# Retention and mixer kernel: 28 causal masks as ScalarE copies with a GpSimd select, 13 sums moved to GpSimd, and another instruction order

## The chip, the cores and the metric

The kernel runs on one core of one Trainium2 chip. A core has a matrix engine (TensorE, PE in the profile), a vector engine (VectorE, DVE), an activation engine (ScalarE, ACT), a general engine (GpSimd, POOL) and a queue engine (SyncE, SP). Each takes its own instructions strictly in the order in which they were written, and waits at an instruction whose inputs are not there. The metric is the device time of one execution in microseconds (us). The time before is the median of three runs, 188.34 us (188.1 to 188.44).

## What is computed

Two layers follow each other. The first is a recurrent retention over 4 batches, 8 heads, 768 positions and head size 64; the second is a token and channel mixer with a 256-wide token part and a 1536-wide channel part.

```python
for t in range(S):
    state = gamma[None, :, None, None] * state + np.einsum('bhd,bhe->bhde', k[:, :, t], v[:, :, t])
    y[:, :, t] = scale * np.einsum('bhd,bhde->bhe', q[:, :, t], state)
...
xt = x.transpose(0, 2, 1)
h = np.maximum(xt @ w_tok1, 0.0) @ w_tok2
u = x + h.transpose(0, 2, 1)
h2 = np.maximum(u @ w_ch1, 0.0) @ w_ch2
return (u + h2).astype(np.float32)
```

`x` is `y` with the heads side by side, 768 x 512 per batch. Inputs, weights and the output are float32.

## The kernel before

The recurrence is computed in chunks of 128 positions. Within a chunk, scores of keys against queries are masked so that a query sees no later key; between chunks a decayed state is carried. The front part (`front(b, p)`) runs once per batch and pair of heads, 16 times. It scales k by the decay (L343, L345), turns q and k (L377, L379, or a transposing transfer, L367), makes the state sums (L408, L418, L420) and their diagonal blocks (L434, L436), the scores (L453), the masks (L463), the products of masked scores with v and of queries with the state (L474, L483), and then the token part of the mixer (L489 to L541), which leaves `u` as float16 for the next products and as float32 in `X`.

A lot of scores is three chunks of one head, a PSUM bank of 128 x 384 float32. A pair has four lots. VectorE multiplies each by the 0/1 mask and writes float16 `am` (L463); six `am` buffers go round. Two lots together feed one group of L474.

The back part (`back(b)`) runs once per batch and is the channel part. Batches 0 and 1 widen with plain products (L606, evicted at L622 by ScalarE); batches 2 and 3 with seven instead of eight block products (`widen7`, L647 to L725). All narrow with seven products where two row blocks are taken together (`narrow7`): sums of blocks (L784), products into three banks (L820 `chain`, L830 `tail`), three partial results kept in SBUF (`us`, L810, "keep"), and adds into `X` (L837, "add"). Of the adds, some read a bank (`FROM_BANK`), one reads one kept quarter (`y11`, 128 x 256, `FROM_KEPT`), and one reads two kept quarters at once (`y2`, 128 x 512). When its adds are done a row block is sent out (L862). Batch 3 ends with two plain blocks (L746, L755, L761).

The order of everything is written out beforehand: `PLAN` is a string, and `placed` reads it. An operation is two base-62 digits, its number in the order of creation; then a digit if it has several possible engines ("ways"), then one digit for each PSUM bank that it takes. A `+` with a digit stands for that many filler matmuls on zeros (L935). Engines, banks and order thus all come from the string; each engine's queue is the string cut down to its own operations. GpSimd's queue holds the requests of weights and of batch 0 and 1's inputs (L257, L292, L295) and casts of v (L360).

Of the kernel before, what the change touches and what calls it, by code (L numbers as in the profile page):

```python
# [11 lines left out]
ALU = mybir.AluOpType  # L12
# [9 lines left out]
class Op:  # L22
# [15 lines left out]
DIGITS = "0123456789abcdefghijklmnopqrstuvwxyzABCDEFGHIJKLMNOPQRSTUVWXYZ"  # L38

PLAN = (  # L40
    "000b09010704020f0d1h00a031i10506+e1n0+31l11o1j20e1p081m1q0c1W31X1k0+31w121A1v451r1x1S0+42x30g1T1+21U41V0+42642"
    "1y0h0k1s2y1z0i2730292t11B51Y11t01Z1E61u02b2u00j201C281F2v21D0212w0+42H242a2c0222J232z32K1G02A240+12I212501H41I"
    "2L2d0m1J02f22g0l2B2M2C2e03812h02D2E390n0p2Q43413511N2i32F02G02j1K2k02N12O0r2P12l2R1L01O01M13630E2o3a72m03712T5"
    "2S02n01P00q2U3b2p03c3d3e2V03i033L61Q53k3f2q03g03j023l3h03n3m0u0o2W2X02Z0t3M2r33o20s3p2Y03013r00v3q03s4k13H13t0"
    "3I11R03u63v2s13w04l3273J53300x3x3A3N70w5s33y03D13B03F3z10z0yaC23C0aF03G13E0aDbc1bdbe5taEbf33O3K0bg3P3Qbl6bh311"
    "3R4g13S4h1aGbi2bmaHbn3V57413W3Y4m33Z0A3T04nbjaL0aMbk4i4aI2aNaJ4300F3X4074j04o3U1aK4u4156bA2410D0C0B4p444q4wbB"
    "4x4rbCb91b05b1421451b32ba4634P0b24Q14y474804v4T64V44cbJ3494a0bKb44s14Ubb4b0bL1d4W4X4R6b54YaU54S14C1aO7aP5o04d0"
    "aQbr3b624z6b74Z1f504t1b8bsaX74f4e14AaV4B0aR24DaS0G511aY521btaW535304aTaZbx21e4F74E154570Kby0I5p0bM4G4H0bu4bG5"
    "bvbo7bw565q04IbzbHbD25r0bNbO550H4J015bEbS0bQ31716bPbFbIbp0R5b55c602582bq59c8184Lcc7bR1bT5a05d04K05e45f5g1620"
    "4M04N01b631cd00L5Y0ce6bX0bY5Z0bV5hbW0c9cb5u15i065466bZch640J4O617M16A2cf67c005v5j07N0ci0685wcac4c1695x5k5yc25z"  # L50
    "5l0cl5m0cu5C10266a0N5Dcv5Ecy5cA4cj1cB0M6b0cm06C05A0cz1c5cq5F5H4cD5B05I6c0cE05Gcr6d62306gck5K75J05LcH5M05N36D0"
    "5O6hcn5P05Q5ncwcx0S0Q5R06f6l3c36ecI15TcF26m5U0cG5W6cM5X15V06EcN6y16i76j6z0dL6cJdq5cK5S1cocZ0dMdU27K16BdVdrcQ1"
    "dscRd84dNdW781cL19d96k1d00Pdk26F6790cS0OdR5dS6G6H6Id16n06JbU6K6o06p1ada1ccT46q0dO10T6L1dPcU6rdl7I17c0dQdT6s07b"
    "6t1d51dm7d16M07a2d6dw56N72066ud76Qdb16O6Rdcdd7J00VdX0dYdZ6P6v17edF76V18i1dn2dxdycV6W7O7f07g7P6dG6S56T8j0dHdo"
    "dh46U0di7hcg7icW77j6X07k6Y07Q7R6Z7Sdp7Ldz27l07008m1cpdjdAdB6w1cX717217T0U731cY74de2dfdg7n7340dt5du7U7p750d22d3"
    "7r7o8n06xdv760d47qdI07X75367v4e07s20X7V081e2e17m0dC18k2807YdD7t7wdJdE7W17u07x0dKeb67y1eIeJeK7Z1geceL7z850e470W"
    "7A08U00Ye507E7Be617C07F0e9cs18258o8S1eO3e38T0cCef837G07D0868Z2eg8l8W18p4ea0908qed7He79112840eM68818reP8s870e8"
    "89ee0ei8X18t92938a08e8ueh8beN08c08VeT177eU8d094ej8f0eRemeQes5eS0eteVen8x72438zeq5eo8h8Yc61eXeW09w08B11ct113er0"
    "8v08y9x00Z10a428AeYf0f19u2evew0f4epex7f5ey8w0ezf86cP08g0eueA0c708C18D970432989bf9eBfc8F08GeCfm28E0999aeD8I7f6"
    "fdcO08H0eEfa3fb8J950eFf7eZfnfo48K0961fffgfe78LfqfD5fh9c3fkfrfpfEa218M0ftfH9dfifAfja319y8N0fl9s19t19f49g9v149e0"  # L60
    "f219h08Ofu8P0fs68R9i18Q1fv9jfF79k0fy9lfGa90aa9z1fz9o9A9m0fIabfw9Bac9C9p09q0gm7fx9DadfKfJ2gnfR4fLgqfP9Eae9n0fS"
    "f319H0316fCfM9L9KfVfNfQg85fT69F0go1fO9Ja5grfWgtfX2fYgpfU9Ig9gs1gugcfZgvg09G0ge6ga0gbg5g39M3gAgdg6gfgy9Na60gggh"
    "9P09O09Qg1g2gwgxg79R0gkgigja709S29TgCfB9U0glgzg4gDgH19Y9VgI19W0gJ5gBgFgKgEaf0gZh34a89Z09X0gO7h0ah3526ajala1ai"
    "h40gMel09rh8gN0eH0gPh1akgQa01h90hcag0am3anha6ao0ap2gGhd1as0aqek0ar0gR1gSgVhbh2heathhau0avaw0hlgThmhfayhnh56az0"
    "hoh6h7hghp0hHax0hr3hw6hq0gWhxgLhuhZ1aBhshv0gUhAhL3i0ig7hyhIhMhti3hN5hihBgX0hz0hPhChKhDi4i6hOihhQhF0hJiki16ii5"
    "iu4hSi2ijidi7i56hR5ibhEhTilhUi8hXinhVicaA0hYiL0im1hWi9j55ioisipiaiviZ3ieiw2itiqiMirixiyizj17j0iN6iPgY0iBj3iQj4"
    "iIiOj2iR2iA6iSk67iCiDeG1jdiTj6j7iGjY1j8iJjbiXiUjeiHiEiYjcifjCj9jG4jEjajZk7k8iViFhj1hk1iWiKk0jfjgjN5k9jk2kahG0"
    "k1kbk2k3jDjOjRke6jH0jLjM0jijr3k4kckd1jPjFjl0jhjSk50jpjq0jI5jQ1jTjW1jsjJjtjvjjjKjwju0jm5jxjUjnjVjojykfkgkhjA0"
    "jX0kijzjB0kjkkkl0"
)  # L70


# [24 lines left out]
def kernel(  # L97
# [11 lines left out]
    nc = tc.nc  # L109
# [48 lines left out]
    def dve(n, per=1.04, extra=0):  # L158
        t = int(65 + extra + n * per)
        return t, t + 83  # L160
# [153 lines left out]
    def front(b, p):  # L314
# [37 lines left out]
        if b in PLAIN:  # L352
            VF, V = V, Slot("v")

            def emit(e):
                t = tile_of(V, [P, 2, NC, D], F16)
                if e == "ACT":
                    nc.scalar.copy(t, VF.tile)
                else:
                    (nc.vector if e == "DVE" else nc.gpsimd).tensor_copy(t, VF.tile)  # L360
# [97 lines left out]
                    [SC[g] for g in run], [KT, QT], tiled="row")  # L458
            score_ops.update({g: a2 for g in run})
        for g, lot in enumerate(lots):  # L460
            def emit(g=g, m=len(lot)):
                am = tile_of(AM[g], [P, m, P], F16)
                nc.vector.tensor_tensor(am, SC[g].tile[:, :m * P].rearrange("p (i t) -> p i t", t=P),  # L463
                                        mask.to_broadcast([P, m, P]), ALU.mult)
# [121 lines left out]
    def back(b):  # L586
# [178 lines left out]
        def narrow7(i0, i1):  # L765
# [14 lines left out]
            for j, (x, y, f, d, prev) in enumerate(sums):  # L780
                def emit(e, j=j, x=x, y=y, f=f):
                    if HS.tile is None:
                        tile_of(HS, [P, 4, K2, P], F16)
                    (nc.vector if e == "DVE" else nc.gpsimd).tensor_tensor(HS.tile[:, j], x(), y(), f)  # L784
# [50 lines left out]
            def add(dst, b_, deps, uses, ways):  # L835
                def emit(e):
                    (nc.vector if e == "DVE" else nc.gpsimd).tensor_tensor(dst(), dst(), b_(), ALU.add)  # L837
# [130 lines left out]
```

## Time and profile before

| | us |
|---|---|
| median of three runs | 188.34 |
| the profiled execution's own time | 188.52 |
| its span, first to last instruction | 186.7 |
| ScalarE's busy time | 122.1 |
| GpSimd's busy time | 33.6 |

The granted TensorE clock was 1.000. In the profile a line such as "L463 DVE TENSOR_TENSOR am<-bank,mask ... x64 | 33.4, 552 | 1.5" is a group: line of the code, engine, operation, what it writes and reads, how many; then busy time in us, the mean length of one in ns, and the engine's idle time just before them. The chain is followed back from the last instruction, at each step to what released it. A stretch row of the view by stretches has the stretch, its length, then for each engine its busy time and in brackets its instructions. Matmuls overlap in the pipeline, so the time that each adds is read from the distance of their starts.

### The profile page before, as it was taken

The page shows a single profiled execution, that of the slowest core. Times are in us where ns is not written, and L with a number is a line of the kernel's source. Part 1 is how long each engine was busy: PE and PEld are TensorE (multiplying, and loading weights), DVE is VectorE, ACT ScalarE, POOL GpSimd, SP SyncE. Part 2 cuts the span into 40 slices and gives each one's busy share as a digit, 9 for nine tenths or more (in the row PEclk, how much of TensorE's full clock was granted, in tenths as well). Part 3 has the DMA queues.
Part 4 walks back from the last instruction along what each step waited for, and adds up shares of the span by engine and source line. Part 5 has one row for each costly group of instructions (what it writes and reads, how often), then busy time and mean ns, then how long its engine had stood idle before and what let it go on. Part 6 is the DMA issues. An engine that isn't in the chain of part 4 may idle for free.

```text
span 186.7 us, 5207 instructions
## 1 busy us (share of the span) xinstructions
PE 178.8 (96%) x2075; PEld 134.9 (72%) x2075; DVE 167.7 (90%) x434; ACT 122.1 (65%) x279; POOL 33.6 (18%) x44
## 2 busy tenths in 40 slices
PE   7888999999999899999999999999999999999992
PEld 3445988677679779765768888776588986566782
DVE  3799998899999799889889999999999999879982
ACT  3837998856779676287988667689875254882110
POOL 8995676420001010001010000021000000000000
PEclk9999999999999999999999999999999999999999
DMA  8999999999999999999999959997926344011025
GB/s 113 154 171 195 178 176 178 185 187 205 190 183 217 183 230 167 148 226 205 131 228 234 162 101 215 312 192 171 157 42 146 111 140 185 2 58 58 32 112 197
DMA packets 94233, 30.23 MB, mean 162 GB/s; under 512 B 84352, under 2 KB 91264, under 8 KB 94208
## 3 DMA queue, kind: packets, MB, share of 16 engines
q1 hardware_dynamic: 61840, 17.63, 53.6%
q0 software_dynamic: 30208, 8.46, 43.8%
q10 hardware_dynamic: 2160, 3.80, 5.6%
q8 instruction: 16, 0.26, 0.6%
q14 instruction: 9, 0.07, 0.1%
HBM read 26.74 MB, written 6.29 MB: 177 GB/s over the span
## 4 chain that ended last, share of the span: by engine, by line
PE 59%; DVE 25%; DMA 6%; ACT 6%; issue 2%; POOL 0%; DVEq 0%; POOLq 0%; ACTq 0%
PE bank L606 15%; PE bank L820 9%; PE bank L679 9%; PE bank L830 7%; DVE am L463 5%; DVE X L837 4%; DMA row<-in_q_dram 4%; PE bank L503 4%; PE bank L523 3%; DVE U L420 3%; DVE hs L784 3%; PE bank L746 3%; DVE h L696 3%; DMA v<-in_v_dram 2%; PE bank L453 2%
## 5 line engine op out<-in xcount | busy, mean ns | idle before, releaser
L606 PE MATMUL bank<-uT,wc 128*128 128x384 f16 x192 | 36.4, 326 | 0.0
L463 DVE TENSOR_TENSOR am<-bank,mask 128x384 f16<-128x384 f32 x64 | 33.4, 552 | 1.5 <-PE bank L453 1.4
L622 ACT ACTIVATE h<-bank 128x384 f16<-128x384 f32 x48 | 22.0, 500 | 10.0 <-PE bank L606 9.8
L606 PEld LDWEIGHTS <-wc 128*128 128x128 f16 x192 | 17.3, 98 | 9.1 <-issue 0.2
L696 DVE TENSOR_TENSOR h<-bank,us 128x384 f16<-128x384 f32 x36 | 18.8, 553 | 2.0 <-ACT us L691 1.0
L691 ACT COPY us<-bank 128x384 f32<-128x384 f32 x36 | 16.6, 484 | 6.1 <-PE bank L679 2.2
L820 PEld LDWEIGHTS <-hs 128*128 128x128 f16 x198 | 18.8, 98 | 2.5
L810 ACT COPY us<-bank 128x256 f32<-128x256 f32 x26 | 9.6, 374 | 16.2 <-PE bank L820 13.8
L360 POOL CAST v<-row 128x768 f16<-128x768 f32 x6 | 5.0, 826 | 82.9 <-DMA row<-in_v_dram 53.6
L837 DVE TENSOR_TENSOR X<-X,bank 128x256 f32<-128x256 f32 x44 | 17.9, 417 | 1.0 <-PE bank L830 0.9
L420 DVE SCALAR_TENSOR_TENSOR U<-U,gp,bank 128x64 f32<-128x64 f32 x64 | 16.8, 278 | 0.8
L820 PE MATMUL bank<-wsum,hs 128*128 128x256 f16 x132 | 17.2, 273 | 0.0
L529 ACT CAST u<-bank 128x384 f16<-128x384 f32 x29 | 13.7, 491 | 4.1 <-PE bank L523 3.4
L679 PE MATMUL bank<-hs,wsum 128*128 128x384 f16 x72 | 15.1, 326 | 0.1
L434 ACT ACTIVATE diag<-U,gp 64x320 f16<-64x320 f32 x24 | 13.3, 559 | 2.6 <-DVE U L420 2.3
L523 PE MATMUL bank<-h,wt 128*128 128x128 f16 x192 | 14.8, 219 | 0.0
L489 ACT CAST x<-bank 128x384 f16<-128x384 f32 x27 | 12.2, 488 | 3.0 <-PE bank L483 2.9
L503 PE MATMUL bank<-x,wt 128*128 128x128 f16 x192 | 13.8, 219 | 0.2 <-DVE U L418 0.2
L830 PEld LDWEIGHTS <-h 128*128 128x128 f16 x132 | 12.5, 98 | 1.9
L679 PEld LDWEIGHTS <-wsum 128*128 128x128 f16 x96 | 9.1, 98 | 5.7 <-issue 0.4
L503 PEld LDWEIGHTS <-wt 128*128 128x128 f16 x192 | 11.9, 98 | 1.9 <-DMA wt<-in_moe_w_tok_dram 0.4
L523 PEld LDWEIGHTS <-wt 128*128 128x128 f16 x192 | 12.1, 98 | 1.2
(91 smaller groups left out, 364.4 us busy)
## 6 DMA issues: line engine op xcount, KB each, us to landing
out_dram<-X ACTq DMA_DIRECT2D x14, 256.0 KB, 2.3
row<-in_q_dram SPq DMA_DIRECT2D x8, 384.0 KB, 4.9
row<-in_v_dram SPq DMA_DIRECT2D x8, 384.0 KB, 5.1
row<-in_k_dram SPq DMA_DIRECT2D x8, 384.0 KB, 5.5
wc<-in_moe_w_ch_dram POOLq DMA_DIRECT2D x5, 512.0 KB, 13.3
out_dram<-X SPq DMA_DIRECT2D x9, 256.0 KB, 3.2
v<-in_v_dram POOLq DMA_DIRECT2D x8, 192.0 KB, 9.3
row<-in_q_dram POOLq DMA_DIRECT2D x8, 192.0 KB, 8.6
```

What stands on the lines that cost most here:

```text
L420: nc.vector.scalar_tensor_tensor(out=u[:, c], in0=u[:, c - 1], scalar=gp[:, p:p + 1], in1=st, op0=ALU.mult, op1=ALU.add)
L463: nc.vector.tensor_tensor(am, SC[g].tile[:, :m * P].rearrange("p (i t) -> p i t", t=P), mask.to_broadcast([P, m, P]), ALU.mult)
L503: nc.tensor.matmul(acc[:, jt * P:(jt + 1) * P], wt1[:, i, jt * P:(jt + 1) * P], X16.tile[:, i], start=(i + jt == 0), stop=(i == NC - 1), s ...
L523: nc.tensor.matmul(Y[hf].tile[:, i * P:(i + 1) * P], wt2[:, jt, t], H1.tile[:, jt], start=False, stop=(jt == NJ - 1), skip_group_check=True)
L606: nc.tensor.matmul(acc[:, :SH], wc1[:, ct, ft * P:(ft + 1) * P], UT.tile[:, ct, sh * SH:(sh + 1) * SH], start=(ct == 0), stop=(ct == NP - 1))
L622: nc.scalar.activation(H2.tile[:, ft], A.tile[:, :SH], AF.Relu)
L679: nc.tensor.matmul(acc[:, :SH], left(ct), r[:, ct], start=first and ct == 0, stop=ct == 1, skip_group_check=True)
L691: (nc.scalar.copy if e == "ACT" else nc.vector.tensor_copy)(kept(j), A.tile[:, :SH])
L696: nc.vector.tensor_tensor(into(hf)[:, ft], bank.tile[:, :SH], kept(j), ALU.add)
L820: nc.tensor.matmul(acc_[:, lo], l[:, j], r[:, j], start=first and j == 0, stop=j == K2 - 1, skip_group_check=True)
L830: nc.tensor.matmul(acc_[:, lo], l[:, j], r[:, j], start=first and j == 0, stop=j == K2 - 1, skip_group_check=True)
L837: (nc.vector if e == "DVE" else nc.gpsimd).tensor_tensor(dst(), dst(), b_(), ALU.add)
```

## The change

For batches 1 to 3 (`CHOSEN`) each of the 48 masks gets two ways: VectorE's product as before, or a plain copy by ScalarE from the bank to `am`, followed by a GpSimd operation that sets the later keys to zero in place (`affine_select`). For a mask that the plan leaves to VectorE, GpSimd's operation puts out no instruction. The readers of `am` now depend on that second operation. The adds of kept results (`y11`, `y2`) get GpSimd as a second way.

The plan is another string throughout. Read with `placed`'s rules, it gives 28 of the 48 masks to ScalarE with GpSimd (9, 7 and 12 in batches 1, 2 and 3), and 13 adds of kept results to GpSimd: 7 of one quarter and 6 of two. Of the other operations that can run on either, 48 go from ScalarE to VectorE and 35 from VectorE to ScalarE (decays, diagonals, evictions); among the casts of v, two go from GpSimd and two to it. Filler matmuls are 45 instead of 35. Six output transfers go from ScalarE's queue to SyncE's, two the other way.

```diff
@@ PLAN @@
-    "000b09010704020f0d1h00a031i10506+e1n0+31l11o1j20e1p081m1q0c1W31X1k0+31w121A1v451r1x1S0+42x30g1T1+21U41V0+42642"
...
+    "00010302050406090b1h00f1i108070d+e1j01k11n11o0a1p1q0e1r1S01s+51l01m0h+71v011W21T11x1y+51Y11w031t01u01X1Z0c0g"
...
@@ settings @@
+    CHOSEN = (1, 2, 3)
@@ front @@
-            def emit(g=g, m=len(lot)):
+            by = []
+
+            def emit(e, g=g, m=len(lot), by=by):
                 am = tile_of(AM[g], [P, m, P], F16)
-                nc.vector.tensor_tensor(am, SC[g].tile[:, :m * P].rearrange("p (i t) -> p i t", t=P),
-                                        mask.to_broadcast([P, m, P]), ALU.mult)
-            am_ops.append(op(one("DVE", dve(len(lot) * P), emit), [score_ops[g], mask_op], [AM[g]], [SC[g]]))
+                sc = SC[g].tile[:, :m * P].rearrange("p (i t) -> p i t", t=P)
+                by.append(e)
+                if e == "ACT":
+                    nc.scalar.copy(am, sc)
+                else:
+                    nc.vector.tensor_tensor(am, sc, mask.to_broadcast([P, m, P]), ALU.mult)
...
+            am_ops.append(op(either(emit, DVE=dve(len(lot) * P), ACT=act(len(lot) * P)), [score_ops[g], mask_op],
+                             [AM[g]], [SC[g]]))
+
+            def emit(g=g, m=len(lot), by=by):
+                if by[0] == "ACT":
+                    nc.gpsimd.affine_select(out=AM[g].tile, in_=AM[g].tile, pattern=[[0, m], [1, P]],
+                                            compare_op=ALU.is_ge, fill=0.0, base=0, channel_multiplier=-1)
+            am_ops[-1] = op([("POOL", 600, 700, emit)], [am_ops[-1]], [], [AM[g]])
+            am_ops[-1].chosen_by = am_ops[-1].deps[0]
@@ narrow7 @@
-            FROM_BANK, FROM_KEPT = dict(DVE=(331, 414)), dict(DVE=(335, 418))
+            FROM_BANK, FROM_KEPT = dict(DVE=(331, 414)), dict(DVE=(335, 418), POOL=(660, 760))
...
-                     dict(DVE=(606, 690)))
+                     dict(DVE=(606, 690), POOL=(1220, 1320)))
```

More of the change, by code (lines that the diff above doesn't have):

```diff
@@ L46 @@
[L46 to L60, printed above, removed]
@@ L66 @@
[L66 to L69, printed above, removed]
+    "00010302050406090b1h00f1i108070d+e1j01k11n11o0a1p1q0e1r1S01s+51l01m0h+71v011W21T11x1y+51Y11w031t01u01X1Z0c0g"
+    "1U41V00k2t0+42642201A210l222u01z2735282x623291E01B41C0i2b2y3812c22v51F392a2402502w01D00j3402d0m0n+32H562J2K2z1"
@@ L70 @@
+    "jL5iUjhjcjdiViWjyiXjkjN7jMjR1jz6jOjljAjBjPji7jniZjQjCjjjm6jSjD7jejoiYjEhK1j1jsjTjFjtkK4jJjZj0jfjKjXjpjujvjUjV"
+    "jqkLjGjYk0jrkoir1fO1f70jwjWjHkS5kTkUkVl06kWkMkNks1jIkOkt0k1k2kqkpkPkxk3k67kQk70kR1i51k4kXk5kz4kd0ky0kYkAkZ1kB"
+    "ku5kC1kDkekbkc0kEkvkrkhkfkg0kGk85kikF0kw1kkl1l2l3kj1kHk9kI0kJ0ka1km0kll4l5kn0l6l70"
 )
@@ L460, in front @@
         for g, lot in enumerate(lots):
-            def emit(g=g, m=len(lot)):
+            by = []
+            def emit(e, g=g, m=len(lot), by=by):
                 am = tile_of(AM[g], [P, m, P], F16)
-                nc.vector.tensor_tensor(am, SC[g].tile[:, :m * P].rearrange("p (i t) -> p i t", t=P),
-                                        mask.to_broadcast([P, m, P]), ALU.mult)
-            am_ops.append(op(one("DVE", dve(len(lot) * P), emit), [score_ops[g], mask_op], [AM[g]], [SC[g]]))
+                sc = SC[g].tile[:, :m * P].rearrange("p (i t) -> p i t", t=P)
[4 more added lines that the diff above has]
+                    nc.vector.tensor_tensor(am, sc, mask.to_broadcast([P, m, P]), ALU.mult)
+            if b not in CHOSEN:
+                am_ops.append(op(one("DVE", dve(len(lot) * P), lambda f=emit: f("DVE")), [score_ops[g], mask_op],
+                                 [AM[g]], [SC[g]]))
+                continue
+            am_ops.append(op(either(emit, DVE=dve(len(lot) * P), ACT=act(len(lot) * P)), [score_ops[g], mask_op],
+                             [AM[g]], [SC[g]]))
+            def emit(g=g, m=len(lot), by=by):
[4 more added lines that the diff above has]
+            am_ops[-1].chosen_by = am_ops[-1].deps[0]
         Y = [Slot(FA) for _ in range(2)]
```

34 lines of the change are left out of this document (25 added, 9 removed).

## The prediction

> **What bounds the kernel now.** I read the page first: its span, the busy shares, then the chain that ended last.
>
> ```profile
> span 186.7 us, 5207 instructions
> ...
> PE   178.8 (96%) x2075; PEld 134.9 (72%) x2075; DVE 167.7 (90%) x434; ACT 122.1 (65%) x279; POOL 33.6 (18%) x44
> ...
> PE 59%; DVE 25%; DMA 6%; ACT 6%; issue 2%; POOL 0%; DVEq 0%; POOLq 0%; ACTq 0%
> ```
>
> TensorE looks full, VectorE stands at 90%, and a quarter of the last chain is VectorE. So the first question is which of the two sets the time. A matmul's shown length includes its pipeline, so busy time says little; the spacing of matmuls in unbroken runs says more. The chain in order of time has such runs, the first wide matmuls of the back part, and VectorE's stretch:
>
> ```profile
> 31.46 3.72 PE bank L606 x22
> ...
> 71.51 0.67 PE bank L503 x12
> ...
> 76.76 3.90 PE bank L606 x24
> ...
> 97.25 0.56 DVE hs L784
> ...
> 98.27 0.93 DVE hs L784 x2
> 99.20 0.93 DVE am L463 x2
> ...
> 132.29 0.47 DVE h L696
> ...
> 141.45 0.44 PE bank L453 x12
> ...
> 179.71 1.31 PE bank L830 x12
> ```
>
> A 384-column matmul costs 3.90/24 = 0.163 us of TensorE, a 256-column one 1.31/12 = 0.109, a 128-column one 0.67/12 = 0.056, a score 0.44/12 = 0.037; a mask or a six-block sum costs VectorE 0.93/2 = 0.465, less than its shown length. Next, how many matmuls there are after 40 us, when the loads are over: the busy time by stretch for L606, L679, L820, L830, L503 and L523 alone, one row each in this order.
>
> ```profile
> 40.00:186.70 146.70, 29.39 (x155) 13.71 (x153) 1.00 0.86 160
> ```
> ```profile
> 40.00:186.70 146.70, 30.88 (x168) 15.96 (x168) 1.00 0.86 160
> ```
> ```profile
> 40.00:186.70 146.70, 34.60 (x264) 24.91 (x264) 1.00 0.86 160
> ```
> ```profile
> 40.00:186.70 146.70, 26.19 (x198) 18.78 (x198) 1.00 0.86 160
> ```
> ```profile
> 40.00:186.70 146.70, 10.49 (x144) 9.19 (x144) 1.00 0.86 160
> ```
> ```profile
> 40.00:186.70 146.70, 11.17 (x144) 9.20 (x144) 1.00 0.86 160
> ```
>
> 323 x 0.163 + 462 x 0.109 + 288 x 0.056 = 52.6 + 50.4 + 16.1 = 119.1 us. The smaller groups, from the groups of TensorE between 40 and 183.5 us:
>
> ```profile
> L474 PE MATMUL bank<-v,am 128*128 128x64 f16 x132 | 7.3, 193 | 0.0
> L746 PE MATMUL bank<-wc,h 128*128 128x256 f16 (+1 forms) x36 | 6.5, 308 | 0.0
> L483 PE MATMUL bank<-diag,qT 128*128 128x128 f16 x55 | 6.3, 219 | 0.0
> ...
> L453 PE MATMUL bank<-qT,kT 64*128 64x128 f16 x120 | 5.1, 217 | 1.3 <-DVE U L420 0.7 <-DVE X L539 0.4 <-PE bank L483 0.3
> ```
>
> By columns these are about 3.7 (half of a 128-column one each), 5.2 (24 of 256 columns, 12 of 512), 3.1 and 4.4, and for the groups left out I put 3.4: 20 us. Together 139 us of work in a stretch of 143.5. So **TensorE is the bound after 40 us and idles about 4.5 us there**, although the chain lies almost wholly on VectorE from 97 to 133 us: other batches' matmuls stand ready and fill in. That caps what relief of VectorE can bring. The change removes no matmul. The rest is the ramp before 40 us, which hangs on loads, and the end:
>
> ```profile
> 183.46 0.42 DVE L755 TENSOR_TENSOR X<-X,bank 128x256 f32<-128x256 f32 x1 [0.51 <-PE bank L746]
> 183.91 0.34 ACTq L761 DMA_DIRECT2D out_dram<-X  x1
> ```
>
> From the last matmul to the end of the span are 3.3 us: an add, an issue, a transfer.
>
> **The change part by part.** The durations, from the groups of instructions by form:
>
> ```profile
> L463 DVE TENSOR_TENSOR am<-bank,mask 128x384 f16<-128x384 f32 x64 | 33.4, 552 | 1.5 <-PE bank L453 1.4
> ...
> L837 DVE TENSOR_TENSOR X<-X,us 128x512 f32<-128x512 f32 x11 | 7.6, 690 | 0.3
> ...
> L837 DVE TENSOR_TENSOR X<-X,us 128x256 f32<-128x256 f32 x11 | 4.6, 422 | 0.1
> ```
> ```profile
> L529 ACT CAST u<-bank 128x384 f16<-128x384 f32 x29 | 13.7, 491 | 4.1 <-PE bank L523 3.4 <-ACT us L810 0.7
> ```
> ```profile
> L360 POOL CAST v<-row 128x768 f16<-128x768 f32 x6 | 5.0, 826 | 82.9 <-DMA row<-in_v_dram 53.6 <-PE bank L523 17.1 <-PE bank L453 10.3
> ...
> L212 POOL IOTA us<- 128x384 f32 x1 | 0.5, 455 | 0.0
> L192 POOL IOTA away<- 128x128 f32 x1 | 0.2, 228 | 0.4 <-POOLq L952 0.4
> ```
>
> *VectorE.* 28 masks of 0.552, 7 quarter sums of 0.422 and 6 half-row sums (two quarters each) of 0.690 leave: 15.5 + 3.0 + 4.1 = 22.6 us, or about 19.1 when each gives 0.087 back to its neighbour, as the mask does (0.552 against 0.465). The new plan also moves evictions and scalings between ScalarE and VectorE: 48 to VectorE, 35 back, net 13, some 5.4 us at 0.42. VectorE's net relief is near 14 us.
>
> *ScalarE.* 28 copies of a 384-column bank at 0.49 are 13.7 us, less 13 leaving operations of about as much each, 6.4: 122 becomes 129 of 187. It has room; a copy frees the score bank as early as the mask did.
>
> *GpSimd, the select.* No row shows one. Its floor is the 384-column iota, 0.455 us. The two iotas give 0.114 + 0.89 us per 1000 columns, and the cast beyond that fixed part (0.826 - 0.114)/768 = 0.93; index and data one after the other make 0.114 + 384 x 1.82/1000 = 0.81. I take 0.6. *The sums.* One operand at the cast's rate is 0.35 for 256 columns and 0.59 for 512 (0.83 for 768 is the row); two operands one after the other 0.59 and 1.06. I take the upper ends, as both operands come through one engine. 28 x 0.6 + 7 x 0.59 + 6 x 1.06 = 27.3 us; GpSimd goes from 34 to 61 us. The Trainium skill, "GPSIMD Engine Reference", section Elementwise — side-by-side cycle accounting, gives about 2.6 cycles per element for two inputs; an estimate by it is 0.67 and 1.22 us, 1.5 us more over the 13 sums, and no run here shows one yet.
>
> *What is queued behind.* After a copy the select waits on GpSimd's own queue, behind weight and batch-1 load issues until 40 us, later behind casts and sums, and TensorE's in-order queue waits at L474 for it. In the new list, TensorE work between the end of the scores and the reader of a chosen mask is at least 2.3 us (by the planner's matmul costs, close to the spacings above), and between the place of the copy and that reader at least 1.5; copy and select need 0.49 + 0.6 = 1.1, so each fits if nothing stands in front. Nine of the 28 selects are listed within 0.7 us of their reader. There I charge 0.07 us on average, 0.6 in all; at worst they lose 0.6 each, 5.4. The sums are waited for by output transfers only, and by the last transfers of batch 3.
>
> *The shared lock.* While a cast ran, VectorE was held twice. First row of each pair GpSimd, second VectorE:
>
> ```profile
> 66.17 0.83 POOL L360 CAST v<-row 128x768 f16<-128x768 f32 x1 [7.47 <-DMA row<-in_v_dram]
> ```
> ```profile
> 66.42 0.98 DVE L784 TENSOR_TENSOR hs<-hs,h 128x768 f16<-128x768 f16 x1
> ```
> ```profile
> 84.12 0.83 POOL L360 CAST v<-row 128x768 f16<-128x768 f32 x1 [17.13 <-PE bank L523]
> ```
> ```profile
> 84.11 1.04 DVE L345 TENSOR_SCALAR k<-row,gk 128x384 f16<-128x384 f32 x1
> ```
>
> The sum at 66.42 ended at 67.40, 0.41 after the cast at 67.00: it had waited for it, for about 0.43 (such a sum beside it is 0.93/2 plus overlap, 0.55). The scaling lost about 0.6. Masks and bank adds beside other casts kept their length. Two of six casts cost VectorE 1.0 us, 0.17 per cast. 41 more instructions, somewhat shorter, make some 6 us; VectorE's net relief falls from 14 to 8. The Trainium skill, "SBUF — State Buffer", section Who interferes with whom, says that VectorE instructions with two SBUF inputs, and its two-port modes, exclude GpSimd's reads for a whole instruction, first come first served; that speaks against this change and the two rows agree with it.
>
> *Fillers and tail.* The plan has 45 filler matmuls for 35; 10 x 0.163 = 1.6 us in the ramp, counted at nothing where TensorE waits for loads, 1.6 if not. In the tail three GpSimd sums (0.59 + 1.06 + 0.59 = 2.2 us) must be done before ScalarE's queue may issue the last transfer. By the list their inputs are ready about 5, 2.5 and 1.3 us before the last matmul ends; run in that order they end before it: nothing, at worst 0.6.
>
> *Sum.* Of the 4.5 us that TensorE idles after 40 us, I give half to VectorE's lateness: -2.3. Late selects: +0.6. Ramp and tail: 0. Net -1.7 us on the span, 185.0. The profiled execution took 188.52, 1.8 more than its span, so 186.8; it lies 0.2 above the median of 188.34, so **186.6 us** for the median.
>
> **The rivals.** (1) *Late selects: slower.* GpSimd's queue becomes a latency in front of TensorE. If a select takes 1.0 instead of 0.6, or a 1.06 us sum stands in front of it, the nine tight ones lose 0.4 to 0.6 us each: 9 x 0.5 = 4.5, less the 2.3 gained, is +2.2, 190.5. It decides when GpSimd's part exceeds about 0.9 us. For: TensorE's queue is in order and full. Against: GpSimd now idles 82% of the span, and the selects may run ahead of their place in the list. (2) *The lock, slower.* Were every one of the 41 to hold a VectorE instruction for its whole length, as two casts did for half to three quarters of theirs, VectorE would lose 27 us and gain 14: 13 us worse than now. TensorE hides most of it (now it idles 4.5 us while VectorE is a quarter of the chain, 47 us); a quarter, 3 us, would show: 191.3. Against: four of six casts held nothing. The Trainium skill's rule on that page is this rival's mechanism. (3) *Nothing.* The 4.5 us idle are transfers and hand-offs, not VectorE's load (the L453 row names a VectorE U, a VectorE X and TensorE itself, 0.3 to 0.7 us each); then -0.3 to +0.3, 188.3. (4) *More.* The new order also tightens the ramp, and most of the 4.5 us go: -4.3, 184.0. That the select is left out cannot be: the place of each select asks which engine the copy was given.
>
> **How the numbers follow.** Forecast (-0.4 to -3.0 us, 185.3 to 187.9) 0.45; late selects 0.22; lock 0.09; nothing 0.14; more 0.10. A measurement of this kernel tells about 0.2% (0.38 us) from no change. Faster: 0.45 + 0.10 and a little of nothing, 0.56; within 0.2%: 0.11; slower 0.22 + 0.09 and a little of nothing, 0.33. The range leaves out the far part of "more" and the upper part of the two slow cases: 184.1 to 190.3. The likeliest case alone is 185.3 to 187.9.
>
> **What would show it.** Right: VectorE's busy time near 150 us, GpSimd's near 61, a select of 0.45 to 0.8 us; TensorE's first wide matmul (L606, now 31.5 us) unmoved, and its idle time after it about 2 us less; VectorE no longer the chain from 97 to 133 us; some VectorE sums of double length beside GpSimd instructions. Wrong: waits of L474 for GpSimd above 1 us in all, an end more than 3.6 us behind the last matmul, or a ramp that is longer by the fillers.

## The result and the profile after

The changed kernel takes 194.76 us (median of 4 runs, 194.7 to 195.4) against 188.22 us for the kernel before in the same rounds (187.86 to 188.44): the ratio is 1.0362, 95% interval 1.0341 to 1.0382. It is 6.5 us slower. The forecast was 186.6 us with a range up to 190.3; the sign was wrong and the time lies outside the range. Of three kernels below some executions were slow (one of E4, two of E14, and one of E9, the profiled one, at a granted clock of 0.659), so their times are medians of the other three, two and three.

The page of the profiled execution (194.76 us), its span, busy shares, last chain and the groups that the change touches (its lines have moved by up to 20: masks L472, copies L470, selects L482, products of masked scores with v L494, first wide products L626, adds L857):

```profile
span 193.1 us, 5305 instructions
...
PE 180.7 (94%) x2085; PEld 135.9 (70%) x2085; DVE 163.9 (85%) x406; ACT 127.6 (66%) x294; POOL 64.9 (34%) x85
...
PE 55%; DVE 22%; DMA 9%; ACT 7%; issue 4%; POOL 0%; DVEq 0%; ACTq 0%; POOLq 0%
...
L482 POOL TENSOR_SCALAR_AFFINE_SELECT am<-am 128x384 f16<-128x384 f16 x28 | 16.5, 606 | 58.3 <-ACT am L470 56.6
...
L472 DVE TENSOR_TENSOR am<-bank,mask 128x384 f16<-128x384 f32 x36 | 18.6, 547 | 2.5 <-PE bank L455 2.3
...
L470 ACT CAST am<-bank 128x384 f16<-128x384 f32 x28 | 13.2, 490 | 1.1 <-PE bank L455 0.8
L804 DVE TENSOR_TENSOR hs<-h 128x768 f16<-128x768 f16 x18 | 11.3, 635 | 2.5 <-ACT h L642 1.8
```

The span grew by 6.4 us. The select came out at 0.606 us, GpSimd at 64.9 us and ScalarE at 127.6, all close to the forecast. VectorE did not: 163.9 us where about 150 was named (the forecast's own net relief of 8 us would give 160), and the block sums L804, plain work that the change does not touch, take 635 ns each where the same group of the kernel before takes 554:

```profile
L784 DVE TENSOR_TENSOR hs<-h 128x768 f16<-128x768 f16 x18 | 10.0, 554 | 0.9 <-ACT h L622 0.5 <-issue 0.2 <-PE bank L820 0.2
```

GpSimd itself is 0% of the last chain, so the loss does not show there as a wait for it.

The groups of GpSimd by form show the sums, which the forecast took at 1.06 and 0.59 us:

```profile
L857 POOL TENSOR_TENSOR X<-X,us 128x512 f32<-128x512 f32 x6 | 8.4, 1406 | 8.1 <-DVE X L857 8.1
...
L857 POOL TENSOR_TENSOR X<-X,us 128x256 f32<-128x256 f32 x7 | 6.7, 956 | 37.7 <-DVE X L857 21.4 <-PE bank L410 9.3 <-ACT u L549 7.0
```

TensorE's waits, longest in all first (what waited, for what, us in all, times, longest):

```profile
PE bank L494 <- DVE am L472: 1.9, 1, 1.9
...
PE bank L626 <- ACT h L642: 1.1, 1, 1.1
PE bank L455 <- DVE X L857: 0.7, 1, 0.7
```

No row names a select: L494 waited for a mask of VectorE, never for GpSimd. So nothing here shows the forecast's first rival, late selects; experiment E10 tests it. Where the wait of 1.9 us comes from is seen in the order of time. VectorE, GpSimd and the waiting matmul between 96 and 105 us (start, length, engine, instruction, in brackets its wait):

```profile
96.60 2.81 POOL L857 TENSOR_TENSOR X<-X,us 128x512 f32<-128x512 f32 x2
...
96.91 1.37 DVE L937 TENSOR_TENSOR wsum<-wsum,wc 128x768 f16<-128x768 f16 x1
...
98.67 1.16 DVE L804 TENSOR_TENSOR hs<-h 128x768 f16<-128x768 f16 x1
...
99.37 0.84 POOL L482 TENSOR_SCALAR_AFFINE_SELECT am<-am 128x384 f16<-128x384 f16 x1
...
99.75 0.87 DVE L804 TENSOR_TENSOR hs<-hs,h 128x768 f16<-128x768 f16 x1
...
102.42 0.82 POOL L362 CAST v<-row 128x768 f16<-128x768 f32 x1
...
102.66 1.12 DVE L857 TENSOR_TENSOR X<-X,us 128x512 f32<-128x512 f32 x1
...
103.71 1.01 DVE L472 TENSOR_TENSOR am<-bank,mask 128x384 f16<-128x384 f32 x2
...
104.31 0.33 PE L494 MATMUL bank<-v,am 128*128 128x64 f16 x6 [1.86 <-DVE am L472]
```

Read the VectorE rows against the GpSimd row above each. The weight sum takes 1.37 us beside two GpSimd sums, the block sums 1.16 and 0.87 beside the second of them and a select, and VectorE's own add of two quarters 1.12 beside a cast. Without GpSimd beside them these take 0.55, 0.55, 0.55 and 0.69 (rows of experiment E10 below). That is 2.2 us in 7 us of time (0.4 of it beside the cast, which the kernel before has too), and the masks behind them reach TensorE late. The masks themselves keep their length, 547 ns on average: of their two inputs one is a PSUM bank.

The stretches from 100 to 140 us show TensorE's busy time (the first busy number; the last columns are granted clock, DMA share and GB/s). First the kernel before, then the changed one:

```profile
100.00:120.00 20.00, 20.00 (x259) 17.44 (x256) 19.87 (x54) 13.66 (x34) 0.00 (x0) 1.00 0.95 197
120.00:140.00 20.00, 19.88 (x221) 14.14 (x219) 19.77 (x54) 16.91 (x42) 1.65 (x2) 1.00 0.83 152
```
```profile
100.00:120.00 20.00, 17.86 (x239) 16.00 (x237) 19.45 (x47) 12.50 (x30) 8.89 (x11) 1.00 0.60 113
120.00:140.00 20.00, 18.71 (x207) 12.62 (x206) 18.96 (x45) 15.78 (x38) 5.89 (x9) 1.00 0.81 201
```

TensorE was full there before and now idles 2.1 and 1.3 us, in the stretches in which GpSimd went from 0.0 and 1.65 us to 8.9 and 5.9.

A kernel with another order can't be compared by stretches alone, since other work lies in them. So each trace was also read by **work done**: the time at which TensorE has started N us of matmuls (fillers left out, each matmul counted by the spacings of the prediction, and the small ones for which it has none, state sums and turns of q, by estimates of 0.02 and 0.028 us). The changed kernel and E10 and E12 have one order, so their rows compare the same matmul. Times in us; E10 and E12 are experiments below, both with the changed order.

| N | before | changed | E10: selects and sums only write | E12: no selects, no sums, a decay moved |
|---|---|---|---|---|
| 25 | 40.78 | 41.36 | 41.24 | 41.26 |
| 30 | 46.00 | 47.97 | 47.88 | 46.92 |
| 50 | 67.31 | 68.71 | 68.62 | 67.65 |
| 80 | 98.85 | 100.19 | 99.67 | 99.01 |
| 85 | 103.82 | 107.77 | 105.26 | 104.43 |
| 100 | 119.27 | 123.97 | 120.77 | 119.88 |
| 125 | 145.09 | 151.46 | 146.86 | 145.80 |
| 160 | 180.31 | 186.65 | 182.06 | 180.99 |

There are two losses. One of 2.0 us is there at N = 30, before 48 us. The other begins at 80 and has grown to 5.0 us (6.4 less the 1.3 of N = 80) at 125; behind that nothing is lost. In E10, whose selects and sums only write, it is 1.0 us, so some 4 of the 5.0 hang on what they read.

### The profile page after: what moved, and what is told of

Its sections match the earlier page's. It is cut to its first block, busy times and chain, and to the rows that moved or that the text cites. A ratio compares the mean times of both kernels' runs of the same rounds, so it can differ in the third digit from the quotient of the medians.

```text
span 193.1 us, 5305 instructions
## 1 busy us (share of the span) xinstructions
PE 180.7 (94%) x2085; PEld 135.9 (70%) x2085; DVE 163.9 (85%) x406; ACT 127.6 (66%) x294; POOL 64.9 (34%) x85
## 4 chain that ended last, share of the span: by engine, by line
PE 55%; DVE 22%; DMA 9%; ACT 7%; issue 4%; POOL 0%; DVEq 0%; ACTq 0%; POOLq 0%
PE bank L699 13%; PE bank L840 10%; PE bank L626 8%; PE bank L850 8%; DMA row<-in_k_dram 8%; PE bank L523 4%; PE bank L543 4%; DVE hs L804 3%; DVE am L472 3%; DVE X L857 3%; PE bank L766 3%; DVE U L422 2%; DVE qT L389 2%; DMA us<-in_k_dram 2%; DVE hs L667 2%
## 5 line engine op out<-in xcount | busy, mean ns | idle before, releaser
L626 PE MATMUL bank<-uT,wc 128*128 128x384 f16 x192 | 36.4, 326 | 1.2 <-ACT h L642 1.1
L482 POOL TENSOR_SCALAR_AFFINE_SELECT am<-am 128x384 f16<-128x384 f16 x28 | 16.5, 606 | 58.3 <-ACT am L470 56.6
L857 POOL TENSOR_TENSOR X<-X,us 128x256 f32<-128x256 f32 (+1 forms) x13 | 15.0, 1164 | 45.8 <-DVE X L857 29.5
L642 ACT ACTIVATE h<-bank 128x384 f16<-128x384 f32 x48 | 22.0, 494 | 7.3 <-PE bank L626 7.1
L626 PEld LDWEIGHTS <-wc 128*128 128x128 f16 x192 | 17.4, 98 | 10.7 <-issue 1.7
L472 DVE TENSOR_TENSOR am<-bank,mask 128x384 f16<-128x384 f32 x36 | 18.6, 547 | 2.5 <-PE bank L455 2.3
L857 DVE TENSOR_TENSOR X<-X,bank 128x256 f32<-128x256 f32 x44 | 17.7, 413 | 3.4 <-PE bank L850 2.3
L840 PE MATMUL bank<-wsum,hs 128*128 128x256 f16 x132 | 17.7, 273 | 0.7 <-DVE us L830 0.4
L543 PEld LDWEIGHTS <-wt 128*128 128x128 f16 x192 | 12.5, 98 | 2.5 <-issue 0.8
L345 ACT ACTIVATE k<-row,gk 128x384 f16<-128x384 f32 (+1 forms) x17 | 10.3, 615 | 5.8 <-DMA row<-in_k_dram 5.7
L850 PEld LDWEIGHTS <-h 128*128 128x128 f16 x132 | 12.5, 98 | 2.2 <-issue 0.6
L470 ACT CAST am<-bank 128x384 f16<-128x384 f32 x28 | 13.2, 490 | 1.1 <-PE bank L455 0.8
L804 DVE TENSOR_TENSOR hs<-h 128x768 f16<-128x768 f16 x18 | 11.3, 635 | 2.5 <-ACT h L642 1.8
```

Source lines behind the costliest of these rows:

```text
L472: nc.vector.tensor_tensor(am, sc, mask.to_broadcast([P, m, P]), ALU.mult)
L543: nc.tensor.matmul(Y[hf].tile[:, i * P:(i + 1) * P], wt2[:, jt, t], H1.tile[:, jt], start=False, stop=(jt == NJ - 1), skip_group_check=True)
L626: nc.tensor.matmul(acc[:, :SH], wc1[:, ct, ft * P:(ft + 1) * P], UT.tile[:, ct, sh * SH:(sh + 1) * SH], start=(ct == 0), stop=(ct == NP - 1))
L642: nc.scalar.activation(H2.tile[:, ft], A.tile[:, :SH], AF.Relu)
L840: nc.tensor.matmul(acc_[:, lo], l[:, j], r[:, j], start=first and j == 0, stop=j == K2 - 1, skip_group_check=True)
L850: nc.tensor.matmul(acc_[:, lo], l[:, j], r[:, j], start=first and j == 0, stop=j == K2 - 1, skip_group_check=True)
```

## The experiments

Two theories could explain the loss, and they can both be part of it. **The lock:** GpSimd's selects and sums hold VectorE while they read, and the held instructions are those that TensorE needs. **The order:** the new plan is slower by itself, with or without GpSimd. A third one, **lateness**, says that GpSimd delivers masks or sums too late, so that its queue and not the lock costs time. Kernels that were timed together share their runs of the kernel before (medians 187.97 to 188.28 us), so ratios are given to those.

### E1 to E3: the new order with the work back on VectorE

The plan's digit for the engine is set back for the 28 masks, for the 13 sums, or for both; the order stays. One mask (entry `4B`) and one sum (entry `cP`) as an example:

```diff
-    "...64EbK470bL4B14X048..."
+    "...64EbK470bL4B04X048..."
-    "...8o17Q1et7PcP1ep7u0..."
+    "...8o17Q1et7PcP0ep7u0..."
```

E1, both:

> The new order and engines, but all 48 masks and all 13 sums on VectorE, so that GpSimd has neither selects nor sums. Lock theory (GpSimd's instructions hold VectorE, and TensorE ends up waiting): the 42 us of GpSimd's work are gone, VectorE carries some 19 us more, no VectorE instruction is stretched; 189 to 190.5 us. Order theory (the new order itself is worse on the chip, whatever GpSimd does): stays at 193.5 us or more.

E2, the masks alone:

> The new order; the 28 masks back on VectorE, the 13 sums stay on GpSimd. Lock theory: the sums are the longer holders (up to 1.4 us each), so about half of the loss stays: 190.5 to 193. Select theory (TensorE waits for late selects): the loss goes, 188 to 189.5. Order theory: 193.5 or more.

E3, the sums alone:

> The new order; the 13 sums back on VectorE, the 28 copies with selects stay. Lock theory: the waits at 97 to 105 us and at 119 to 128 us go, as they stand beside sums; 190 to 192. Select theory: unchanged, 194 or more. Order theory: 193.5 or more.

| | us | ratio to before (95%) | VectorE busy | GpSimd busy |
|---|---|---|---|---|
| changed kernel | 194.76 | 1.0362 (1.0341 to 1.0382) | 163.9 | 64.9 |
| E1 both on VectorE | 208.15 | 1.1079 (1.1029 to 1.1129) | 175.5 | 34.5 |
| E2 masks on VectorE | 205.61 | 1.0942 (1.0889 to 1.0994) | 173.9 | 50.0 |
| E3 sums on VectorE | 197.63 | 1.0492 (1.0437 to 1.0548) | 165.5 | 51.5 |

With the sums back VectorE is only 1.6 us busier than in the change, and the kernel is 2.9 us slower; with the masks back it is 10.9 us slower. E1 lies where the order theory put it, at 193.5 us or more, but so far above the change itself that neither theory explains it; E2 does too, and E3 fits the order theory and the one of late selects alike. TensorE's longest wait in E1:

```profile
PE bank L850 <- DVE am L472: 5.4, 3, 2.5
```

L850 does not read `am`; what it can wait for is the bank that a late mask still has to read. The order is built round the copies: with the masks on VectorE, TensorE stands at L850, and everything behind it in its queue stands too. The granted clock was lower as well in E1, 0.973 on average. Putting work back therefore measures the order's fit, not the lock. The right question is what the GpSimd work costs in its own order, and for that it has to be taken out, not put back.

### E4 and E14: the old order with the GpSimd work

E4 takes the plan of before, gives the same 28 masks to ScalarE with the select listed right behind, and the 13 sums to GpSimd. E14 is E4 with two casts of v, those of the last two pairs of heads of batch 3 (entries `aM2` and `a82`), moved behind the selects. The edit from E4 to E14:

```diff
-    "...ab00Z10aM298199fKfMfNa82fhfi0fQ...9K09L9M19Nfp09i7f..."
+    "...ab00Z1098199fKfMfNfhfi0fQ...9K09L9M19NaM2a82fp09i7f..."
```

> The order of before, with the same 28 masks as ScalarE copies with a select (put right behind the copy) and the same 13 sums on GpSimd; nothing else of the change. Lock and select theories: GpSimd's work costs what it costs in any order, 191 to 195. Order theory: 187 to 189.

> The order of before with the 28 copies and selects and the 13 sums, as in the earlier run of 202.4 us, but the two casts of v of batch 3 that stood in GpSimd's queue ahead of selects, one of them waiting 7.5 us for its transfer, are put behind the selects of pairs 0 and 1. If the select's wait behind the cast is the 5.3 us wait of TensorE there: 196.5 to 199. If TensorE waits for something else in that stretch: 201.5 to 203.

E4 took 201.66 us, ratio 1.0737 (1.0676 to 1.0798), above both expectations, with VectorE at only 154.9 us. Its longest wait of TensorE, and then the rows in the order of time that explain it:

```profile
PE bank L494 <- POOL am L482: 6.5, 2, 5.3
```
```profile
125.37 0.82 POOL L362 CAST v<-row 128x768 f16<-128x768 f32 x1 [7.47 <-DMA row<-in_v_dram]
126.14 0.52 POOL L482 TENSOR_SCALAR_AFFINE_SELECT am<-am 128x384 f16<-128x384 f16 x1
...
126.72 0.50 PE L494 MATMUL bank<-v,am 128*128 128x64 f16 x6 [5.26 <-POOL am L482]
```

This is a queue and not a lock: GpSimd stood 7.47 us at a cast whose input had not landed, and the select behind it, 0.52 us long, kept TensorE for 5.26. It is the forecast's first rival, and it happens in the old order, not in the new one.

E14 took 200.45 us, 1.0649 (1.0615 to 1.0684), between its two expectations: the 5.3 us wait is gone, and only 1.2 us of the time (1.7 by the ratios). Waits of E14, and its rows:

```profile
PE bank L699 <- ACT us L711: 5.0, 2, 4.3
PE bank L494 <- POOL am L482: 1.2, 1, 1.2
```
```profile
124.48 0.82 POOL L362 CAST v<-row 128x768 f16<-128x768 f32 x1 [3.09 <-DMA row<-in_v_dram]
...
127.39 0.83 POOL L362 CAST v<-row 128x768 f16<-128x768 f32 x1 [2.08 <-DMA row<-in_v_dram]
128.18 1.26 POOL L857 TENSOR_TENSOR X<-X,us 128x512 f32<-128x512 f32 x1
129.48 0.48 ACT L711 COPY us<-bank 128x384 f32<-128x384 f32 x1 [4.44 <-POOL X L857]
```

Now a sum stands behind the same casts. It holds a `us` buffer until it has read it; ScalarE waits 4.44 us for the buffer and TensorE for ScalarE. The sums were not "waited for by output transfers only", as the prediction had it: who waits for the buffers that they read is a waiter too. These two runs don't price the lock in the old order, since waits in queues of up to 5.3 us lie over it.

### E5, E6, E7: the changed kernel without its new GpSimd work

Same order, same copies on ScalarE. E5 is without the selects and the sums, E6 without the selects, E7 without the sums.

```diff
@@ E5, E6 @@
-                if by[0] == "ACT":
+                if False:
                     nc.gpsimd.affine_select(...)
@@ E5, E7 @@
-                    (nc.vector if e == "DVE" else nc.gpsimd).tensor_tensor(dst(), dst(), b_(), ALU.add)
+                    if e == "DVE":
+                        nc.vector.tensor_tensor(dst(), dst(), b_(), ALU.add)
```

> The new order with ScalarE's 28 copies, but without the 28 selects and without the 13 sums (28 lots stay unmasked, and 13 kept results are not added to X): everything else, order and engines included, as in the change. Lock theory (GpSimd's selects and sums hold VectorE's instructions, or come late themselves): the whole loss goes, 187 to 189 us. Order theory (new order alone): 193 to 195.

> As the change, without the 28 selects (28 lots stay unmasked). If the loss at 42 to 46 us comes from selects that stand in GpSimd's queue ahead of load requests, it goes (1.4 us), and so does that at 145 to 151 us (0.9 us), where four selects hold VectorE; the two at 97 to 105 and 119 to 128 us stay, as they stand beside sums: 191.5 to 193. If selects alone make the loss: 188.5.

> As the change, without the 13 sums (13 kept results are not added to X). If the sums' hold on VectorE makes the losses at 97 to 105 us (2.6 us) and 119 to 128 us (1.7 us): 190 to 191.5. If selects alone make the loss: 194.5.

| | us | ratio to before (95%) | VectorE busy | GpSimd busy |
|---|---|---|---|---|
| E5 neither | 190.41 (11 runs) | 1.0102 (1.0075 to 1.0130) | 157.1 | 33.9 |
| E6 sums only | 191.05 | 1.0129 (1.0071 to 1.0187) | 161.3 | 48.9 |
| E7 selects only | 190.96 | 1.0126 (1.0064 to 1.0189) | 159.7 | 50.4 |

The line of E5's page, with VectorE's relief in full:

```profile
PE 180.1 (95%) x2085; PEld 135.8 (72%) x2085; DVE 157.1 (83%) x406; ACT 127.3 (67%) x294; POOL 33.9 (18%) x44
```

E5 lies between its two expectations, so neither theory is the whole; E6 is a little below its 191.5 to 193, E7 within 190 to 191.5. Even with no selects and no sums to pay for, this order is 190.41 - 188.28 = 2.1 us slower than before. E5 has the relief and the new order at once; by work done they can be told apart in part. From N = 30 to N = 160 E5's trace takes 134.3 us (48.54 to 182.87), the kernel before 134.3 too, E10 134.2 and E12 134.1. So some 10 us less on VectorE brought 0.0 to 0.2 us there, and nearly all of the order's loss lies before. Whether the old order would gain more by the same relief was not run, nor the new order without the 83 other operations that changed engine.

The GpSimd work costs 194.76 - 190.41 = 4.4 us on top, and 163.9 - 157.1 = 6.8 us of VectorE's busy time, though it does nothing on VectorE. The held time adds up: 161.3 - 157.1 = 4.2 us by the sums alone, 159.7 - 157.1 = 2.6 by the selects alone. Its price doesn't: either part alone costs 0.6 us, both together 4.4. A likely reason, which no run tests, is that a small delay is covered by matmuls that stand ready, and the second finds no cover left.

### E8: the loads first

In the changed kernel GpSimd's first select waits 7.82 us, and load requests of k, v and weights stand behind it. E8 moves that select (entry `41`) behind five requests.

```diff
-    "...10w4r3W00z3X41cqcs3bM6420ctbN..."
+    "...10w4r3W00z3Xcqcs3bM6420ctbN...z04u4A0C3Z0D41cm3cr..."
```

> As the change, but the first select (batch 1, pair 0) is put behind the five load requests that follow it in GpSimd's queue: v and k of batch 1 and three weight pieces. If the idle 7.8 us of GpSimd in front of that select delay the loads and these ScalarE and then TensorE, the step at 42 to 46 us goes: 192.8 to 193.8. If loads are not what is late there: 194.5 to 195.

194.78 us, 1.0325 (1.0265 to 1.0385): nothing. The requests go out some 7 us earlier, and the row of k that ScalarE waits for lands no earlier. The decay that reads it, first in E8, then in the changed kernel, in the order of time:

```profile
44.09 0.61 ACT L345 ACTIVATE k<-row,gk 128x384 f16<-128x384 f16 x1 [1.64 <-DMA row<-in_k_dram]
```
```profile
43.48 0.62 ACT L345 ACTIVATE k<-row,gk 128x384 f16<-128x384 f16 x1 [1.46 <-DMA row<-in_k_dram]
```

The row that this decay reads (its wait and the request name the same semaphore) was not among the five. In the change it had been requested well before the select at 37.57 us, in this row, and landed at 43.45:

```profile
28.70 1.05 POOL L297 DMA_DIRECT2D row<-in_k_dram  x1 [0.45 <-DMA wc<-in_moe_w_ch_dram]
```

The row of k that E8 did move was requested at 32.27 us instead of 39.41 and landed at 46.50 instead of 45.48. So the select in front of the requests was not what made these loads late.

### E9 and E10: GpSimd work that reads nothing

This pair tells the lock from lateness. GpSimd is kept about as busy, at the same places in its queue and with the same waits, but by instructions that only write. In E9 each sum becomes three writes of a quarter or two of a half row; in E10 each select becomes a write too.

```diff
@@ E9, E10 @@
+                    else:
+                        n_ = 2 * N2 if "POOL" in ways and ways["POOL"][0] > 1000 else N2
+                        for _ in range(2 if n_ > N2 else 3):
+                            nc.gpsimd.iota(dst(), pattern=[[1, n_]], base=0, channel_multiplier=0, ...)
@@ E10 @@
-                    nc.gpsimd.affine_select(out=AM[g].tile, in_=AM[g].tile, ...)
+                    nc.gpsimd.iota(AM[g].tile, pattern=[[0, m], [1, P]], base=0, channel_multiplier=0, ...)
```

> As the change, but each of the 13 GpSimd sums is replaced by GpSimd index patterns written to the same part of X, three for a quarter and two for a half row, so that GpSimd is as long in use and waits for the same things but reads no SBUF (13 kept results are not added to X). If it is the reading of SBUF that holds VectorE (the lock): as without the sums, 190.5 to 191.6 us, and no VectorE sum is stretched beside them. If it is GpSimd's time in use, by which selects come late: 194 or more.

> As the run before, and the 28 selects too replaced by an index pattern written to am, which reads nothing (28 lots get indices instead of masked scores). Lock theory: as without any GpSimd work, 189.9 to 191 us; whether the clamp of two blocks (float16 to float16 in SBUF) is still stretched at 146 us is open. Lateness theory: 194 or more.

E9 took 191.68 us, ratio 1.0189 (1.0160 to 1.0219): just above the 190.5 to 191.6 of the lock theory and far below 194. Against E7, which has no sums at all, it is higher by 0.6% with intervals that overlap; whether the writes cost that is open. E10 took 190.32 us, 1.0121 (1.0106 to 1.0136). Its page:

```profile
span 188.6 us, 5317 instructions
...
PE 180.9 (96%) x2085; PEld 136.1 (72%) x2085; DVE 157.8 (84%) x406; ACT 127.2 (67%) x294; POOL 60.4 (32%) x105
...
L482 POOL IOTA am<- 128x384 f16 x28 | 13.0, 482 | 57.2 <-ACT am L470 57.1
L862 POOL IOTA X<- 128x256 f32 (+1 forms) x33 | 13.9, 429 | 43.9 <-DVE X L858 42.6
```

GpSimd is as good as equally busy (60.4 against 64.9 us), with 20 instructions more, and the time is that of E5, which has none of this work (190.32 against 190.41; 2.35 and 2.13 us above their own runs of the kernel before). The same place of the work as in the timeline above:

```profile
96.02 2.33 POOL L862 IOTA X<- 128x512 f32 x4
96.40 0.55 DVE L943 TENSOR_TENSOR wsum<-wsum,wc 128x768 f16<-128x768 f16 x1
...
97.34 0.55 DVE L804 TENSOR_TENSOR hs<-h 128x768 f16<-128x768 f16 x1
97.80 0.55 DVE L804 TENSOR_TENSOR hs<-hs,h 128x768 f16<-128x768 f16 x1
...
100.31 0.69 DVE L858 TENSOR_TENSOR X<-X,us 128x512 f32<-128x512 f32 x1
100.92 1.01 DVE L472 TENSOR_TENSOR am<-bank,mask 128x384 f16<-128x384 f32 x2
```

The four writes of two half-row sums stand beside the weight sum and both block sums, and these keep their 0.55 us. The two masks start at 100.92 instead of 103.71. So it is what GpSimd reads that costs, not that it is busy and not when it is done. The Trainium skill, "SBUF — State Buffer", section Who interferes with whom, says that a VectorE instruction with two SBUF inputs contends with a GpSimd instruction that reads SBUF and not with one that only writes it; this pair of traces agrees, 1.37 against 0.55 us for one weight sum.

### E11, E12, E13: where the order loses

The table by work shows 1.9 us lost before N = 30 in E10 too. There, ScalarE stands at the decay of k shown under E8 and waits for its load, with the evictions of the wide products behind it: TensorE's 1.1 us wait of L626 for L642. E11 moves this decay (entry `4X0`) behind four other ScalarE instructions; E12 does the same in E5; E13 is E12 with the ten extra fillers of the ramp cut.

```diff
@@ E11, E12 @@
-    "...64EbK470bL4B14X048cnco4v4..."
+    "...64EbK470bL4B148cnco4v4...1bBcg1bTbCbU4X0461bQ..."
@@ E13 @@
-    "...00j3402d0m0n+32H562J2K2z12A0r+32I35...02E3662e0+41H12M1I3..."
+    "...00j3402d0m0n2H562J2K2z12A0r2I35...02E3662e01H12M1I3..."
```

> As the change, but ScalarE's decay of k of batch 1, pair 2, which waited 1.5 us for its transfer at 43.5 us, is put behind four ScalarE instructions that TensorE waits for. If it is this wait at the head of ScalarE's queue that makes the step at 42 to 46 us: 1.1 to 1.4 us less there and 193.3 to 193.9 in all, unless a later stretch takes it back. If TensorE waits for something else there: 194.5 to 195.

> The same move of the decay in the kernel without selects and sums (28 lots unmasked, 13 kept results not added). With that wait gone the order alone should be worth 189.0 to 189.6 against 190.4; what is left above before is the ramp. If nothing moves: 190.2 to 190.6.

> The kernel without selects and sums and with the later decay (28 lots unmasked, 13 kept results not added), and the last ten filler matmuls of the ramp cut, so that there are 35 as before. If fillers take TensorE's time in the ramp, it is up to 1.6 us faster than 189.7: 188.1 to 189.2. If TensorE would wait there anyhow: 189.5 to 189.9, and the rest of the order's loss is where its operations stand.

E11: 193.90 us, 1.0330 (1.0295 to 1.0364). E12: 189.71 us, 1.0091 (1.0076 to 1.0106). Each set against its own runs of the kernel before (187.97 here), E11 is 0.6 us better than the change and E12 0.4 better than E5; the intervals of the ratios overlap, so the end of the kernel shows this gain only weakly. In the traces of both, N = 30 comes 0.9 us or more earlier than without the move (47.02 and 46.92 us, against 47.97 in the change, 47.88 in E10 and 48.54 in E5), so one load at the head of ScalarE's queue is 0.9 us of the order's loss at N = 30.

E13: 190.52 us, 1.0113 (1.0084 to 1.0142), against E12's 1.0091: above both expectations, no faster than E12, and with overlapping intervals not clearly slower. The granted clock in 40 slices, E13's first and the changed kernel's second:

```profile
PEclk9999699999999999999999999999999999999998
```
```profile
PEclk9999999999999999999999999999999999999998
```

With the fillers cut, the clock falls to 6 tenths in the fifth slice (about 19 to 24 us); the first wide product starts at 33.5 us instead of 31.9, and N = 25 comes at 42.84 instead of 41.26. Two of E13's four executions had a mean granted clock of 0.987 and took 190.94 and 190.82 us; the other two had 0.998 and 1.0 and took 190.21 and 189.99. So the extra fillers are not what the order loses by: without them the kernel gains nothing, and in two of four executions the clock fell. What is left of the order's loss, 189.71 - 187.97 = 1.7 us, is not settled. By the table E12 is 0.5 us late at N = 25, 0.2 at 80, and 0.6 to 0.7 from 85 on; the two profiled executions differ by 1.1 us only (189.57 and 188.52), and the rest of that lies behind the last row. No further run took it apart.

No kernel of this study is faster than the one before; the best, E12, leaves the selects and sums out and is still 0.9% slower.

## Why the prediction was wrong

**What bounds the kernel: right, but drawn on too far.** TensorE is the bound after 40 us, with the same matmuls in both. The step that failed is the first term of the sum: "Of the 4.5 us that TensorE idles after 40 us, I give half to VectorE's lateness: -2.3." E5 tests this term together with the order. There VectorE has all of its relief (157.1 us instead of 167.7), GpSimd has no new work, and the kernel is 2.1 us slower. Behind N = 30 the relief brought 0.0 to 0.2 us of the 2.3, so on this point the rival "nothing" was right. Before N = 30 the new order, which the sum took as free in the ramp, lost some 2 us, 0.9 of them by a decay in front of a late load. The second step that failed is that the sum has no term for the lock at all: it was put at nothing and measured +4.4. Together 2.1 + 4.4 = 6.5 us, where -1.7 was forecast.

**The lock: the right mechanism, the right size on VectorE by luck, and the wrong sum.** The forecast charged 0.17 us per new GpSimd instruction, "some 6 us", from two held instructions beside six casts. Measured are 6.8 us for 41, 0.166 each, but neither kind has that price: E6 gives 4.2/13 = 0.32 us for a sum, E7 2.6/28 = 0.09 for a select. It was then set against relief, "VectorE's net relief falls from 14 to 8", as if a held microsecond and a saved one were the same goods. They are not: the saved ones lay where TensorE did not wait, the held ones fell on block sums and weight sums with masks for TensorE queued behind them, and 4.4 of the 6.8 came through to the end. The rival with this mechanism counted a quarter of VectorE's loss and had a chance of 0.09; it gave 191.3 us by GpSimd's holds alone. The share that came through was about two thirds (4.4/6.8), and the order's 2.1 came on top. With the sums alone it was 0.15 (0.64 of 4.2) and with the selects alone 0.21 (0.55 of 2.6), so a fixed share is no way to price it. The rival's "against", that four of six casts held nothing, was no sign either: in the trace of before these four stood beside instructions that read a bank, but for two scalings of k at their edges. That GpSimd's reads, and not its lateness, do this is shown by E10 against the change; that the rest of the loss is there without any of this work is shown by E5.

**VectorE's relief: too large.** Near 14 us were expected before the lock, and E5 shows 10.6. The lengths of VectorE's instructions add up to 195.4 us in the trace of before and to 178.8 in E5's: 16.6 less, where 22.6 - 5.4 = 17.2 were forecast. But they overlap by 27.7 us before and by 21.7 in E5, 6.0 less, where 3.6 were forecast (41 times 0.087): with more gaps fewer instructions overlap their neighbour, so the same work counts as more busy time. VectorE is at 85% of a longer span: it is not short of time, it is late at certain places.

**Late selects: not seen in the change.** L494 waited for GpSimd not once. The nine tight selects cost nothing that the waits show; for the 0.6 us charged no run shows anything. E4 shows that the fear was sound for another order (5.26 us behind a cast).

**Costs of single instructions.** The select was taken at 0.6 and is 0.606 (0.52 where VectorE has nothing to hold it). ScalarE: 129 forecast, 127.6 measured. The sums were taken at 0.59 and 1.06 and take 0.956 and 1.406 in this kernel; with nothing beside them they take 0.73 (the shortest in each trace) and 1.26 (the row of E14). The estimate by the Trainium skill, "GPSIMD Engine Reference", section Elementwise — side-by-side cycle accounting, 0.67 and 1.22, is nearer than the one taken: the second operand costs more than the rate of the cast. GpSimd's total of 61 came out at 64.9, mainly for the sums.

**Ramp and tail.** The tail cost nothing, as forecast: the last transfer is issued at 190.25 us, and the end follows the last matmul by as much as before. Fillers at nothing in the ramp: right, since E13 without ten of them is no faster. The first wide product starts at 32.0 us, in the trace of before at 31.3, where "unmoved" was forecast: part of the order's loss.

## What to carry to other kernels

Work given to GpSimd that reads SBUF held VectorE's sums of two SBUF inputs here: ask for each of these who waits for it, and price the hold there, not as a share of VectorE's load. Relief of an engine that is busy 90% of the time can be worth nothing where the bound engine hardly waits for it: look for the waits first, the busy share last. And before moving work to an in-order queue, read what stands ahead of it and which buffers it holds: one cast waiting for its load turned a 0.5 us select into a wait of 5.3 us, and with the cast moved, a sum into one of 4.3.

## What the hardware showed beyond that

- **The hold goes both ways.** A select takes 0.52 us alone and 0.84 in the timeline of the change beside a block sum; a sum of two quarters 1.26 alone and 2.81/2 = 1.41 in a pair beside VectorE's sums. Part of GpSimd's 64.9 us is waiting.
- **Writes alone hold some VectorE work too.** In E10 block sums are untouched, but the clamp of `h` (one float16 input, output in SBUF) is not. Three clamps beside three writes, in the order of time:

```profile
142.04 1.62 POOL L482 IOTA am<- 128x384 f16 x3 [6.16 <-ACT am L470]
142.23 1.64 DVE L745 TENSOR_SCALAR h<-h 128x768 f16<-128x768 f16 x3
```

  The same three clamps in E5, where GpSimd does nothing beside them:

```profile
143.26 0.89 DVE L745 TENSOR_SCALAR h<-h 128x768 f16<-128x768 f16 x3
```

  The Trainium skill, "SBUF — State Buffer", section Who interferes with whom, gives the rule: VectorE's two-port modes shut out GpSimd altogether and are shut out by it, whereas two-input instructions meet only its reads. These rows agree with it if the clamp runs in such a mode, which no row names.
- **The clock.** With ten more fillers of 0.163 us (1.6 us of TensorE's time) the mean granted clock was 0.998 or more in all four executions of E12. Without them it was 0.987 in two of four of E13, about 0.8 us slower than the other two, and in the trace one slice of 4.7 us had 6 tenths.
